# Decoding double-precision weights on VectorE alone, in an attention and maxout kernel on one core

## The chip, the cores and the metric

The kernel runs on one core of one Trainium2 chip. The metric is the device time of one execution in microseconds (us), given as the median of several executions. The engines of the core are TensorE (PE in the profile, its weight loads PEld), VectorE (DVE), ScalarE (ACT), GpSimd (POOL) and SyncE (SP, which here only issues transfers). Each runs its own instructions strictly in its own order and waits on semaphores where it needs another engine's result.

## The reference

The reference is causal attention with a bias from a running sum, and then a feed-forward layer in which the largest of three products is kept:

```python
scores = scale * np.matmul(q, k.transpose(0, 1, 3, 2))      # 8 batches, 8 heads, 576 positions, width 64
s_pos = np.maximum(s, 0.0)
cum = np.cumsum(s_pos, axis=-1)
bias = -(cum[:, :, :, None] - cum[:, :, None, :])
scores = np.where(causal, -1000000000.0, scores + np.minimum(bias, 0.0))
attn = np.exp(scores - np.max(scores, axis=-1, keepdims=True))
attn = attn / (np.sum(attn, axis=-1, keepdims=True) + 1e-09)
x = np.matmul(attn, v)                                      # heads side by side: 4608 tokens of 512
h = np.maximum(np.maximum(x @ w1, x @ w2), x @ w3)          # 512 to 768
out = h @ w_out                                             # 768 to 512
```

The four weight matrices are drawn in double precision, and lie in memory as 64-bit words.

## The kernel before

**The steps.** Attention runs in 160 steps. A step is one block of 128 queries (64 in the last block of a sequence) of one pair of heads; a visit is a run of steps of one pair. Visits 0 to 7 (two batches, four pairs) take query blocks 0 and 1, which is phase 0; so steps 0 to 15 are the even and odd steps of eight visits. Visits 8 to 15 take blocks 2, 3 and 4 of the same pairs (phase 1), and every later visit all five. In step t the engines do, in program order:

- `probs(t)`, first half: DVE takes the reciprocal `ri` (L486), ACT writes the high half `prh` of the probabilities in f16 (L502).
- `highest(t + 1)`: DVE takes the row maximum `nm` (L450) of the next step's scores. Then come the functions put down with `amid` for this step.
- `probs(t)`, second half: DVE writes the low half `prl` (L505), and SP issues two DMA transposes (L508) of `prh` and `prl` into the tiles `ph` and `pl`, from which the product with the values reads.
- the evictions of matmul results (L583, L584, L725, L728), at most one group of feed-forward matmuls, and `scores(t + 2)` on PE (L419, in one of two PSUM tiles `s`), which needs `prl` of step t to be done with its tile.
- `expo(t + 1)` on ACT (L460, L464), which gives `se`, the input of the next `ri`.
- the functions put down with `at` for this step, further feed-forward groups, and `values` (L574) of the visit that ended in the step before.

The order is written out: no engine looks for other work when the next instruction in its row has to wait.

**The weights.** 24 tiles of 128 rows by 512 doubles (18 of w1, w2, w3, 6 of w_out), 512 KB each, are loaded once (`load_w`, L187), four from SP and twenty from ACT. A tile is turned into two f16 halves in these parts, spread over the steps up to 17:

- `decode1` (ACT, L605): the high words, read as f32, times 2^-112 into a tile `t` (three buffers);
- `signs` (POOL, L609): the high words times zero, in place, which leaves only the sign bit;
- `decode2a` (DVE, L613): the low words shifted right by 29, ORed with that sign;
- `decode2b` (DVE, L620): `t` shifted left by 3, ORed with the result, which is the weight in f32;
- `gram1` and `gram2`: a bound for the scale, from all tiles of a kind;
- `decode3` (ACT, L674): the high f16 half; and `decode4`, the low one: DVE in one operation (L684) for 16 tiles, POOL in two (L681, L682) for the 8 tiles whose number is in `LOW`.

In steps 0 to 6 two tiles are decoded a step (one before step 0), in step 7 three, in steps 8 to 13 one. `decode4` of three tiles a step follows in steps 9 to 14, 16 and 17. A feed-forward group of PE (`h_group`, L711; `o_group`, L753) may be issued only in a step after its weights' `decode4`; `run_group` issues them by a budget that is worked out when the program is built, so PE's row is fixed.

**The transposed tiles.** `PT` holds `ph` and `pl` in a pool with one buffer a tag. The first eight visits take the tags `pTh0` and `pTh1` in turns (and `pTl0`, `pTl1`); later ones take the tag of their phase.

**DMA semaphores.** Eight of them (DMAHW0 to DMAHW7 in the rows below) are handed out in turns over all transfers, of SP and ACT alike. A transfer is issued only when the one that held its semaphore before has landed.

The rest of POOL's work around there is the low half of k (`qkl`, L327) and the split of the feed-forward result (`hh` L717, `hl` L718).

Of the kernel before, what the change touches and what calls it, by code (L numbers as in the profile page):

```python
# [8 lines left out]
F32 = mybir.dt.float32  # L9
F32R = mybir.dt.float32r  # L10
F16 = mybir.dt.float16
BF16 = mybir.dt.bfloat16
I32 = mybir.dt.int32
I64 = mybir.dt.int64
AF = mybir.ActivationFunctionType
ALU = mybir.AluOpType
# [5 lines left out]
def kernel(  # L22
# [9 lines left out]
    nc = tc.nc  # L32

    P = 128
    D = 64
    B, NP, _, QKV = qkv.shape
    HB, S = s.shape
    NW, _, N = wts.shape
# [6 lines left out]
    NB = qkv0.shape[0]  # L45
# [6 lines left out]
    PH = [(0, 256), (256, 320)]  # L52
# [4 lines left out]
    LOW = set(range(2, 24, 3))  # L57

    const = ctx.enter_context(tc.tile_pool(name="const", bufs=1))
# [131 lines left out]
    zero = const.tile([P, 1], F32, name="zero")  # L191
    nc.gpsimd.memset(zero, 0.0)
# [276 lines left out]
    def probs(t):  # L469
# [5 lines left out]
        if qb in (0, 2):  # L475
            PT[v, ph] = [
                att.tile(
                    [P, 4 + 4 * ph, PH[ph][1]], F16, tag=f"pT{c}{v % 2 if v < NP * NB else ph}", name=f"p{c}{t}", bufs=1
                )
                for c in "hl"  # L480
            ]
            if ph:
                PT[v, ph].append(att.tile([P, 1, P], F16, tag="tT", name=f"tT{t}"))
# [115 lines left out]
    def words(i):  # L599
        w = raw_w[i].rearrange("p (n t) -> p n t", t=2)  # L600
        return w[:, :, 0], w[:, :, 1]
# [5 lines left out]
    def signs(i):  # L607
        hi = words(i)[1]
        nc.gpsimd.tensor_tensor(out=hi, in0=hi, in1=zero.to_broadcast([P, N]), op=ALU.mult)  # L609

    def decode2a(i):
        lo, hi = (x.bitcast(I32) for x in words(i))
        nc.vector.scalar_tensor_tensor(  # L613
            out=lo, in0=lo, scalar=29, in1=hi, op0=ALU.logical_shift_right, op1=ALU.bitwise_or
        )

    def decode2b(i):
        lo = words(i)[0].bitcast(I32)
        ti = half.pop(i).bitcast(I32)
        nc.vector.scalar_tensor_tensor(  # L620
            out=lo, in0=ti, scalar=3, in1=lo, op0=ALU.logical_shift_left, op1=ALU.bitwise_or
        )
# [53 lines left out]
    def decode4(i):  # L676
        t = words(i)[0]
        w = pairs_w[i // 2][:, i % 2]
        sw = WS["u" if i < 18 else "d"]
        if i in LOW:  # L680
            nc.gpsimd.tensor_tensor(out=t, in0=t, in1=sw.to_broadcast([P, N]), op=ALU.mult)  # L681
            nc.gpsimd.tensor_tensor(out=w[:, 1], in0=t, in1=w[:, 0], op=ALU.subtract)  # L682
        else:
            nc.vector.scalar_tensor_tensor(  # L684
                out=w[:, 1], in0=t, scalar=sw, in1=w[:, 0], op0=ALU.mult, op1=ALU.subtract
            )
        fresh[i] = w.rearrange("p h (a c) -> p h a c", c=P)
# [122 lines left out]
    def at(t, f, *a):  # L810
        todo.setdefault(t, []).append((f, a))
# [15 lines left out]
    fetched = {5: -1, 7: -1, 8: 0, 9: 0, 10: 1, 11: 1, 12: 2, 13: 2, 14: 3, 15: 3, 16: 4, 17: 4}  # L827
    fetched.update({22: 5, 23: 5, 18: 5, 19: 6, 20: 6, 21: 7})
# [13 lines left out]
    parts2 = {}  # L842
    for i, t in sorted(begun.items(), key=lambda x: (x[1], x[0])):
        parts2.setdefault(t + 1, []).append(i)
    for t, ids in parts2.items():
        (amid if t >= 0 else at)(t, decode2a, ids[0])
        for i in ids[1:]:
            at(t, decode2a, i)
        for i in ids:
            at(t, decode2b, i)  # L850
# [46 lines left out]
    for i, t in sorted(begun.items()):  # L897
        at(t, decode1, i)
        at(t, signs, i)
    for n, (i, t) in enumerate(fetched.items()):  # L900
        (amid if t >= 0 and n % 2 == 0 else at)(t, load_w, i, nc.scalar.dma_start)
# [114 lines left out]
```

## Time and profile before

| what | us |
|---|---|
| median of 3 runs | 944.0 (943.08 to 945.74) |
| the profiled execution, its own time | 945.22 |
| its span, first to last instruction | 943.4 |
| PE busy | 838.6 |
| DVE busy | 582.7 |
| ACT busy | 569.4 |
| POOL busy | 386.8 |

The span is 1.8 us less than the profiled execution's time, and that time is 1.2 us above the median. In the profile's rows a group is named by source line, engine, operation and tiles; behind a stroke stand its busy time, the mean duration in ns, and the idle time of the engine just before it with what ended it.

### The profile page before, as it was taken

To read this page: it belongs to the slowest core of one execution; us is meant where nothing else is said; L and a number is where in the kernel's file an instruction comes from. 1 tells how busy PE (TensorE), PEld (TensorE's weight loads), DVE (VectorE), ACT (ScalarE), POOL (GpSimd) and SP (SyncE) were. 2 spreads that over 40 slices of the span, in tenths; PEclk is the share of its full clock that TensorE was granted. 3 is DMA by queue.
4 is the path that set the end of the run, shared out by engine and by line. 5 is a ranking of instruction groups with operands and counts; after the bars stand their busy time and mean duration, and the time that the engine had idled before them with its cause. 6 is when DMAs were issued, how large, how long until landed. Compare 5 with 4: busy or idle time off the path is not lost. (4 is left out here: it accounts for less than half of the span.)

```text
span 943.4 us, 19983 instructions
## 1 busy us (share of the span) xinstructions
PE 838.6 (89%) x7192; PEld 653.2 (69%) x7192; DVE 582.7 (62%) x1184; ACT 569.4 (60%) x1502; POOL 386.8 (41%) x592
## 2 busy tenths in 40 slices
PE   2456768887779899999999998999999999998998
PEld 2444647765556677877887777877887787776876
DVE  6897885666556575667575666576666656563111
ACT  4667566566467576676676676666667666764111
POOL 4455742222433453635453535454455435430211
PEclk9857999999899999999999999999999999999999
DMA  7974236566577678777778677787676676744000
GB/s 277 237 223 88 58 75 140 115 137 150 118 139 144 119 138 162 152 141 136 157 141 155 134 135 135 135 141 145 133 138 148 127 153 102 139 69 96 2 24 28
DMA packets 242035, 122.34 MB, mean 130 GB/s; under 512 B 217808, under 2 KB 226512, under 8 KB 241936
## 3 DMA queue, kind: packets, MB, share of 16 engines
q1 hardware_dynamic: 237904, 108.74, 58.1%
q10 hardware_dynamic: 4032, 12.32, 4.1%
q8 instruction: 57, 0.93, 0.4%
q14 instruction: 42, 0.34, 0.2%
HBM read 60.18 MB, written 9.44 MB: 74 GB/s over the span
## 5 line engine op out<-in xcount | busy, mean ns | idle before, releaser
L711 PE MATMUL pm<-x,w 128*128 128x256 f16 (+1 forms) x3456 | 462.9, 290 | 3.7 <-ACT m L725 1.7
L711 PEld LDWEIGHTS <-w 128*128 128x128 f16 x3456 | 334.2, 99 | 89.6 <-issue 4.1
L505 DVE SCALAR_TENSOR_TENSOR prl<-s,ri,prh 128x512 f16<-128x512 f32 (+3 forms) x288 | 152.8, 567 | 96.6 <-ACT prh L502 50.4
L717 POOL CAST hh<-m 128x256 f16<-128x256 f32 (+1 forms) x96 | 53.5, 557 | 351.4 <-DVE m L728 294.4
L502 ACT ACTIVATE prh<-s,ri 128x512 f16<-128x512 f32 (+3 forms) x288 | 141.8, 538 | 80.8 <-DVE ri L486 71.7
L450 DVE TENSOR_REDUCE nm<-s 128x1 f32<-128x576 f32 (+4 forms) x160 | 128.0, 800 | 49.3 <-PE s L385 28.9
L460 ACT ACTIVATE s<-s,nm 128x512 f32<-128x512 f32 (+4 forms) x288 | 151.2, 525 | 9.2 <-DVE nm L450 4.1
L753 PE MATMUL po<-hh,w 128*128 128x256 f16 (+1 forms) x768 | 150.4, 287 | 1.5 <-DVE w L684 1.5
L728 DVE SCALAR_TENSOR_TENSOR m<-pm,m 128x256 f32<-128x256 f32 (+1 forms) x192 | 87.1, 454 | 97.4 <-PE pm L711 85.0
L753 PEld LDWEIGHTS <-w 128*128 128x128 f16 x1152 | 110.4, 98 | 31.1 <-DVE w L684 2.1
L753 PE MATMUL po<-hl,w 128*128 128x320 f16 (+1 forms) x384 | 110.0, 287 | 0.9 <-POOL hl L718 0.8
L725 ACT ACTIVATE m<-pm 128x256 f32<-128x256 f32 (+1 forms) x96 | 39.1, 407 | 83.9 <-PE pm L711 80.2
L718 POOL TENSOR_TENSOR hl<-m,hh 128x256 f16<-128x256 f32 (+1 forms) x96 | 74.1, 772 | 7.8
L583 ACT ACTIVATE x<-av 128x256 f16<-128x256 f32 (+1 forms) x64 | 26.3, 410 | 78.6 <-PE av L574 77.9
L138 POOL CAST l<-kb 64x576 fp32r<-64x576 f32 x48 | 32.3, 673 | 100.6 <-PE s L394 75.6
L761 ACT ACTIVATE o<-po,os 128x256 f32<-128x256 f32 (+1 forms) x64 | 31.9, 498 | 65.5 <-PE po L753 50.0
L169 POOL TENSOR_TENSOR l<-raw,h 64x576 fp32r<-64x576 f32 x48 | 68.2, 1422 | 7.2 <-ACT h L155 6.0
L584 DVE SCALAR_TENSOR_TENSOR x<-av,x 128x256 f16<-128x256 f32 (+1 forms) x64 | 29.1, 454 | 59.0 <-ACT x L583 58.9
L574 PEld LDWEIGHTS <-vh 128*64 128x64 f16 x832 | 45.0, 112 | 24.6 <-issue 17.1
L574 PE MATMUL av<-pl,vh 128*64 128x320 f16 (+3 forms) x384 | 56.3, 279 | 5.7 <-DMA pl<-prl 5.6
L379 PE MATMUL s<-h 128*128 128x128 f32 (+1 forms) x192 | 53.7, 361 | 8.4 <-DVE prl L505 7.0
L574 PE MATMUL av<-ph,vh 128*64 128x320 f16 (+3 forms) x384 | 57.5, 287 | 0.6 <-DMA ph<-prh 0.6
(142 smaller groups left out, 1148.2 us busy)
## 6 DMA issues: line engine op xcount, KB each, us to landing
raw<-in_qk_dram SPq DMA_DIRECT2D x96, 304.0 KB, 4.7
r<-in_w_dram ACTq DMA_DIRECT2D x20, 512.0 KB, 4.9
rv<-in_qkv_dram SPq DMA_DIRECT2D x32, 320.0 KB, 3.4
out_dram<-o SPq DMA_DIRECT2D x32, 160.0 KB, 2.0
out_dram<-o SPq DMA_DIRECT2D x32, 128.0 KB, 2.3
raw<-in_qkv_dram SPq DMA_DIRECT2D x8, 480.0 KB, 3.9
ph<-prh SPq DMA_TRANSPOSE x192, 3.3
pl<-prl SPq DMA_TRANSPOSE x192, 2.8
```

The lines of the kernel that those rows point to most:

```text
L169: nc.gpsimd.tensor_tensor(out=l[far, QP:V0], in0=raw[far, QP:V0], in1=h[far, QP:V0].bitcast(F32), op=ALU.subtract)
L379: nc.tensor.matmul(ps[:, j, :nk], lhsT=w[:, qs], rhs=w[:, QP:QP + nk], start=(x == "h"), stop=False, skip_group_check=True,)
L450: nc.vector.tensor_reduce(out=nm, in_=sc, axis=AX.X, op=ALU.max, negate=True)
L460: nc.scalar.activation(out=sc, in_=sc, func=AF.Exp, bias=nm[:, j:j + 1], accum_out=sm[:, j:j + 1])
L502: nc.scalar.activation(out=hi, in_=src, func=AF.Copy, scale=sc)
L505: nc.vector.scalar_tensor_tensor(out=lo, in0=src, scalar=sc, in1=hi, op0=ALU.mult, op1=ALU.subtract)
L574: nc.tensor.matmul(av[j * D:(j + 1) * D, c0:nq], lhsT=lt, rhs=rt, start=(n < 2), stop=(n >= len(todo) - 2), skip_group_check=True,)
L711: nc.tensor.matmul(pm[:, :nq], lhsT=w[:, wt, kt, :], rhs=xt, start=(n == 0), stop=(n == 3 * NKT - 1))
L717: nc.gpsimd.tensor_copy(out=st["hh"][:, ft, :nq], in_=m1[:, :nq])
L718: nc.gpsimd.tensor_tensor(out=st["hl"][:, ft, :nq], in0=m1[:, :nq], in1=st["hh"][:, ft, :nq], op=ALU.subtract)
L728: nc.vector.scalar_tensor_tensor(out=m1[:, :nq], in0=pm[:, :nq], scalar=HSC, in1=m1[:, :nq], op0=ALU.mult, op1=ALU.max)
L753: nc.tensor.matmul(pm[:, :nq], lhsT=W[18 + ft][:, wt, dt, :], rhs=st[ht][:, ft, :nq], start=(n == 0), stop=(n == 3 * NFT - 1),)
```

## The change

`signs` and the constant `zero` go, and POOL takes no part in the decode any more. `decode1` stays. `decode2a` and `decode2b` become three operations of DVE: `shift` (`t` shifted left by 3, in place, one input), `low_bits` (the low words shifted right by 29, ORed into `t`) and `sign` (the sign bit of the high words ORed with `t`, written over the low words). All tiles of a step go through one operation before the next: the shifts stand between `nm` and `prl` (`amid`), the other two behind, where before the first tile's `decode2a` alone stood ahead of `prl`. `decode4` is one DVE operation for all 24 tiles. The weight loads are issued earlier, three a step from the start, and always at the step's end. The tiles `ph` and `pl` get one buffer a phase in all visits.

```diff
-    LOW = set(range(2, 24, 3))
...
-    zero = const.tile([P, 1], F32, name="zero")
-    nc.gpsimd.memset(zero, 0.0)
...
-                att.tile(
-                    [P, 4 + 4 * ph, PH[ph][1]], F16, tag=f"pT{c}{v % 2 if v < NP * NB else ph}", name=f"p{c}{t}", bufs=1
-                )
-                for c in "hl"
+                att.tile([P, 4 + 4 * ph, PH[ph][1]], F16, tag=f"pT{c}{ph}", name=f"p{c}{t}", bufs=1) for c in "hl"
...
-    def signs(i):
-        hi = words(i)[1]
-        nc.gpsimd.tensor_tensor(out=hi, in0=hi, in1=zero.to_broadcast([P, N]), op=ALU.mult)
-
-    def decode2a(i):
+    def shift(i):
+        ti = half[i].bitcast(I32)
+        nc.vector.tensor_scalar(out=ti, in0=ti, scalar1=3, scalar2=None, op0=ALU.logical_shift_left)
+
+    def low_bits(i):
+        lo, ti = words(i)[0].bitcast(I32), half[i].bitcast(I32)
+        nc.vector.scalar_tensor_tensor(
+            out=ti, in0=lo, scalar=29, in1=ti, op0=ALU.logical_shift_right, op1=ALU.bitwise_or
+        )
+
+    def sign(i):
         lo, hi = (x.bitcast(I32) for x in words(i))
...
-            out=lo, in0=ti, scalar=3, in1=lo, op0=ALU.logical_shift_left, op1=ALU.bitwise_or
+            out=lo, in0=hi, scalar=-(2 ** 31), in1=ti, op0=ALU.bitwise_and, op1=ALU.bitwise_or
...
-        if i in LOW:
-            nc.gpsimd.tensor_tensor(out=t, in0=t, in1=sw.to_broadcast([P, N]), op=ALU.mult)
-            nc.gpsimd.tensor_tensor(out=w[:, 1], in0=t, in1=w[:, 0], op=ALU.subtract)
-        else:
-            nc.vector.scalar_tensor_tensor(
-                out=w[:, 1], in0=t, scalar=sw, in1=w[:, 0], op0=ALU.mult, op1=ALU.subtract
-            )
+        nc.vector.scalar_tensor_tensor(
+            out=w[:, 1], in0=t, scalar=WS["u" if i < 18 else "d"], in1=w[:, 0], op0=ALU.mult, op1=ALU.subtract
+        )
...
-    fetched = {5: -1, 7: -1, 8: 0, 9: 0, 10: 1, 11: 1, 12: 2, 13: 2, 14: 3, 15: 3, 16: 4, 17: 4}
-    fetched.update({22: 5, 23: 5, 18: 5, 19: 6, 20: 6, 21: 7})
+    fetched = {5: -1, 7: -1, 8: -1, 9: 0, 10: 0, 11: 0, 12: 1, 13: 1, 14: 1, 15: 2, 16: 2, 17: 2}
+    fetched.update({22: 4, 23: 4, 18: 5, 19: 6, 20: 6, 21: 7})
...
+    for t, ids in together.items():
+        for f in (shift, low_bits, sign):
+            for i in ids:
+                (amid if f is shift and t >= 0 else at)(t, f, i)
...
-        at(t, signs, i)
-    for n, (i, t) in enumerate(fetched.items()):
-        (amid if t >= 0 and n % 2 == 0 else at)(t, load_w, i, nc.scalar.dma_start)
+    for i, t in fetched.items():
+        at(t, load_w, i, nc.scalar.dma_start)
```

In DVE's row, step 4 reads like this before, from its `ri` to the next one (r is a weight tile, t its rescaled high words):

```order
L486 RECIPROCAL ri_505<-se_478 128x2
L450 TENSOR_REDUCE nm_464<-s_463 128x2
L613 SCALAR_TENSOR_TENSOR r_299<-r_299 128x512
L505 SCALAR_TENSOR_TENSOR prl_508<-s_378,ri_505,prh_507 128x128 x2
L613 SCALAR_TENSOR_TENSOR r_309<-r_309 128x512
L620 SCALAR_TENSOR_TENSOR r_299<-t_495,r_299 128x512
L620 SCALAR_TENSOR_TENSOR r_309<-t_498,r_309 128x512
L354 SCALAR_TENSOR_TENSOR vl_490<-st_139,inv_0_233,vh_489 128x2x128
L486 RECIPROCAL ri_587<-se_534 128x2
```

The same step in DVE's row after the change (line numbers are those of the changed file):

```order
L480 RECIPROCAL ri_505<-se_481 128x2
L447 TENSOR_REDUCE nm_467<-s_466 128x2
L603 TENSOR_SCALAR t_499<-t_499 128x512
L603 TENSOR_SCALAR t_501<-t_501 128x512
L499 SCALAR_TENSOR_TENSOR prl_508<-s_379,ri_505,prh_507 128x128 x2
L607 SCALAR_TENSOR_TENSOR t_499<-r_295,t_499 128x512
L607 SCALAR_TENSOR_TENSOR t_501<-r_297,t_501 128x512
L614 SCALAR_TENSOR_TENSOR r_295<-r_295,t_499 128x512
L614 SCALAR_TENSOR_TENSOR r_297<-r_297,t_501 128x512
L351 SCALAR_TENSOR_TENSOR vl_494<-st_137,inv_0_231,vh_493 128x2x128
L480 RECIPROCAL ri_587<-se_533 128x2
```

Four operations on two weight tiles have become six; none of them reads anything of POOL's.

In ACT's row, this is the end of step 2 and the beginning of step 3 before, where DMA rows on r are weight loads and those on rv loads of values:

```order
L605 ACTIVATE t_425<-r_252 128x512
L605 ACTIVATE t_428<-r_264 128x512
L187 DMA r_431<-in_w_dram 128x512
L502 ACTIVATE prh_448<-s_315,ri_446 128x2x128 x2
L187 DMA r_454<-in_w_dram 128x512
L583 ACTIVATE x_0_460<-av_0_433 128x256
L460 ACTIVATE s_378,sm_475<-s_378,nm_379 128x128 x2
L464 ACTIVATE se_478<-sm_475 128x2
L112 DMA rv_485<-in_qkv_dram 128x256
L112 DMA rv_487<-in_qkv_dram 128x256
```

And the same place in ACT's row after:

```order
L599 ACTIVATE t_427<-r_248 128x512
L599 ACTIVATE t_429<-r_250 128x512
L186 DMA r_431<-in_w_dram 128x512
L186 DMA r_433<-in_w_dram 128x512
L186 DMA r_435<-in_w_dram 128x512
L496 ACTIVATE prh_452<-s_314,ri_450 128x2x128 x2
L577 ACTIVATE x_0_463<-av_0_437 128x256
L457 ACTIVATE s_379,sm_478<-s_379,nm_380 128x128 x2
L461 ACTIVATE se_481<-sm_478 128x2
L111 DMA rv_489<-in_qkv_dram 128x256
```

Three loads (tiles 15, 16 and 17) now stand in a row ahead of `prh`; before, one stood ahead of it and one behind (tiles 13 and 14).

SP's row holds the same transfers in the same order; its waits differ. These are the four transposes of visit 1 (steps 2 and 3) and the first of visit 2 (step 4) before, each with the semaphores it waits for:

```order
L508 DMA_TRANSPOSE ph_362<-prh_366 128x2x128 [waits DMAHW6_49,Activation_49]
L508 DMA_TRANSPOSE pl_363<-prl_367 128x2x128 [waits DMAHW0_49,DVE_49,PE_49]
L508 DMA_TRANSPOSE ph_362<-prh_448 128x4x128 [waits DMAHW3_49,Activation_49]
L508 DMA_TRANSPOSE pl_363<-prl_449 128x4x128 [waits DMAHW4_49,DVE_49]
L508 DMA_TRANSPOSE ph_503<-prh_507 128x2x128 [waits DMAHW1_49,DMAHW2_49,PE_49,Activation_49]
```

And after:

```order
L502 DMA_TRANSPOSE ph_364<-prh_368 128x2x128 [waits DMAHW4_49,DMAHW3_49,DMAHW6_49,PE_49,Activation_49]
L502 DMA_TRANSPOSE pl_365<-prl_369 128x2x128 [waits DMAHW7_49,DMAHW6_49,DVE_49]
L502 DMA_TRANSPOSE ph_364<-prh_452 128x4x128 [waits DMAHW0_49,Activation_49]
L502 DMA_TRANSPOSE pl_365<-prl_453 128x4x128 [waits DMAHW1_49,DVE_49]
L502 DMA_TRANSPOSE ph_503<-prh_507 128x2x128 [waits DMAHW4_49,DMAHW0_49,DMAHW7_49,PE_49,Activation_49]
```

The first transpose of visit 1 now waits for PE, that is for the last matmul of `values` of visit 0, because both visits write the same buffer. In step 4 the wait for PE stood there before too, but for the visit before the last; now it is for the last one, whose `values` stands at the end of step 4 in PE's row.

More of the change, by code (lines that the diff above doesn't have):

```diff
@@ L605, in decode1 @@
         nc.scalar.activation(out=half[i], in_=words(i)[1], func=AF.Copy, scale=2.0 ** -112)
-    def signs(i):
-        hi = words(i)[1]
-        nc.gpsimd.tensor_tensor(out=hi, in0=hi, in1=zero.to_broadcast([P, N]), op=ALU.mult)
-    def decode2a(i):
-        lo, hi = (x.bitcast(I32) for x in words(i))
-        nc.vector.scalar_tensor_tensor(
-            out=lo, in0=lo, scalar=29, in1=hi, op0=ALU.logical_shift_right, op1=ALU.bitwise_or
-        )
-    def decode2b(i):
-        lo = words(i)[0].bitcast(I32)
+    def shift(i):
[7 more added lines that the diff above has]
+    def sign(i):
+        lo, hi = (x.bitcast(I32) for x in words(i))
         ti = half.pop(i).bitcast(I32)
         nc.vector.scalar_tensor_tensor(
-            out=lo, in0=ti, scalar=3, in1=lo, op0=ALU.logical_shift_left, op1=ALU.bitwise_or
+            out=lo, in0=hi, scalar=-(2 ** 31), in1=ti, op0=ALU.bitwise_and, op1=ALU.bitwise_or
         )
@@ L678, in decode4 @@
         w = pairs_w[i // 2][:, i % 2]
-        sw = WS["u" if i < 18 else "d"]
-        if i in LOW:
-            nc.gpsimd.tensor_tensor(out=t, in0=t, in1=sw.to_broadcast([P, N]), op=ALU.mult)
-            nc.gpsimd.tensor_tensor(out=w[:, 1], in0=t, in1=w[:, 0], op=ALU.subtract)
-        else:
-            nc.vector.scalar_tensor_tensor(
-                out=w[:, 1], in0=t, scalar=sw, in1=w[:, 0], op0=ALU.mult, op1=ALU.subtract
-            )
+        nc.vector.scalar_tensor_tensor(
+            out=w[:, 1], in0=t, scalar=WS["u" if i < 18 else "d"], in1=w[:, 0], op0=ALU.mult, op1=ALU.subtract
+        )
         fresh[i] = w.rearrange("p h (a c) -> p h a c", c=P)
@@ L841 @@
         at(first[v] + 1 if v else -2, vscale2, scale_of(v))
-    parts2 = {}
+    together = {}
     for i, t in sorted(begun.items(), key=lambda x: (x[1], x[0])):
[L844 to L850, printed above, removed]
+        together.setdefault(t + 1, []).append(i)
+    for t, ids in together.items():
+        for f in (shift, low_bits, sign):
+            for i in ids:
+                (amid if f is shift and t >= 0 else at)(t, f, i)
     for i, t in split.items():
@@ L896 @@
         at(t, decode3, i)
-    for i, t in sorted(begun.items()):
+    for i, t in begun.items():
         at(t, decode1, i)
-        at(t, signs, i)
-    for n, (i, t) in enumerate(fetched.items()):
-        (amid if t >= 0 and n % 2 == 0 else at)(t, load_w, i, nc.scalar.dma_start)
+    for i, t in fetched.items():
+        at(t, load_w, i, nc.scalar.dma_start)
     at(1, spread, 1)
```

## The prediction

> **What bounds the kernel now.** I read PE's row of the page's slices first (busy tenths of 40 equal slices), then the busy time of two windows.
>
> ```profile
> PE   2456768887779899999999998999999999998998
> ...
> 12.00:142.00 130.00, 77.02 (x630) 59.73 (x630) 112.11 (x224) 82.47 (x222) 68.95 (x67) 0.82 0.57 146
> 142.00:943.00 801.00, 758.36 (x6550) 591.00 (x6550) 465.07 (x950) 483.12 (x1273) 312.25 (x495) 0.99 0.64 124
> ```
>
> A window's row gives its length, then the busy time of PE, PEld, DVE, ACT and POOL, the granted clock, the DMA share and GB/s. From 142 us on PE is busy for 758 of 801 us: matmul work bounds that part, and the change doesn't touch it. From 12 to 142 us, which is where the weights are decoded, PE is busy for 77 of 130 us and DVE for 112. PE's row is fixed when the program is built, and nothing after 142 us refers to a time, so what the first part gains or loses is passed on whole. Who waits for whom from 12 to 142 us:
>
> ```profile
> ACT prh L502 <- DVE ri L486: 26.0, 12, 5.7
> PE s L419 <- DVE prl L505: 22.4, 7, 5.7
> ...
> DVE r L613 <- POOL r L609: 11.4, 9, 3.4
> ...
> DVE prl L505 <- ACT prh L502: 2.4, 2, 1.7
> ```
>
> Columns: total, times, longest. ACT and PE wait for DVE; DVE itself waits for little but POOL's sign operation. So DVE's row sets the pace of this part, and 130 us are 112 of work, 11.4 of waiting for POOL and small waits.
>
> **The change part by part.** Its operations in that window, and their shortest, median and longest durations:
>
> ```profile
> L613 DVE SCALAR_TENSOR_TENSOR r<-r 128x512 int32<-128x512 int32 x24 | 23.8, 994 | 11.4 <-POOL r L609 11.4
> L620 DVE SCALAR_TENSOR_TENSOR r<-t,r 128x512 int32<-128x512 int32 x24 | 16.9, 734 | 0.1
> L684 DVE SCALAR_TENSOR_TENSOR w<-r,swu,w 128x512 f16<-128x512 f32 x12 | 13.1, 1132 | 0.0
> L684 DVE SCALAR_TENSOR_TENSOR w<-r,swd,w 128x512 f16<-128x512 f32 x4 | 5.6, 1442 | 0.0
> L330 DVE SCALAR_TENSOR_TENSOR qkl<-raw,qkh 128x256 fp32r<-128x256 f32 x4 | 3.7, 918 | 0.0
> L330 DVE SCALAR_TENSOR_TENSOR qkl<-st,qkh 128x256 fp32r<-128x256 f32 x3 | 1.2, 415 | 0.0
> ...
> L613 DVE SCALAR_TENSOR_TENSOR r<-r x24: 676/694/1520, 16.6 to 105.2; 128x512 int32<-128x512 int32 x24
> L620 DVE SCALAR_TENSOR_TENSOR r<-t,r x24: 673/680/1343, 18.2 to 107.8; 128x512 int32<-128x512 int32 x24
> L684 DVE SCALAR_TENSOR_TENSOR w<-r,swu,w x12: 740/1158/1639, 78.1 to 117.5; 128x512 f16<-128x512 f32 x12
> ```
>
> *The wait.* `shift` needs only ACT's `t`, so DVE's 11.4 us of waiting for POOL go. Step 10 shows one such wait, and DVE's row from one `ri` to the next (start, length, idle before in brackets):
>
> ```profile
> 79.75 0.16 DVE L486 RECIPROCAL ri<-se 128x2 f32<-128x2 f32 x1
> 82.17 1.51 DVE L613 SCALAR_TENSOR_TENSOR r<-r 128x512 int32<-128x512 int32 x1 [1.67 <-POOL r L609]
> 84.13 1.12 DVE L620 SCALAR_TENSOR_TENSOR r<-t,r 128x512 int32<-128x512 int32 x1
> 86.50 1.65 DVE L354 SCALAR_TENSOR_TENSOR vl<-rv,inv,vh 128x256 f16<-128x256 f32 x2
> 88.07 0.15 DVE L486 RECIPROCAL ri<-se 128x2 f32<-128x2 f32 x1
> ```
>
> The last `ri` begins at 88.07, 80 ns ahead of the end of L354 at 88.15: of operations that follow each other, each costs some 80 ns less than its length.
>
> *The slow half.* The same operation on the same shape takes 676 ns or 1520. On POOL one operation of one shape, L681, has a mean of 1270 or 1042 ns in its two rows below. I read this as DVE and POOL holding each other up when both are at work. Above the shortest there are 24 x (994 - 676) = 7.6 us on L613, 24 x (734 - 673) = 1.5 on L620, 12 x (1132 - 740) + 4 x (1442 - 740) = 7.5 on L684, and 4 x (918 - 415) = 2.0 on `qkl`, by its two rows: 18.6 us. POOL's work in the window is 68.95 us, and what goes is this:
>
> ```profile
> L609 POOL TENSOR_TENSOR r<-r,zero 128x512 f32<-128x512 f32 x24 | 28.2, 1190 | 34.2 <-ACT t L605 34.1
> L682 POOL TENSOR_TENSOR w<-r,w 128x512 f16<-128x512 f32 x8 | 11.2, 1398 | 0.6
> L681 POOL TENSOR_TENSOR r<-r,swu 128x512 f32<-128x512 f32 x6 | 7.6, 1270 | 0.0
> L681 POOL TENSOR_TENSOR r<-r,swd 128x512 f32<-128x512 f32 x2 | 2.1, 1042 | 1.2 <-ACT w L674 1.2
> ```
>
> That is 49.1 of 68.95 us, 71%. I take the hold-ups to go with POOL's time: 0.71 x 18.6 = 13.2 us; the bounds are 0 and 18.6.
>
> *The added operations.* `low_bits` and `sign` have two inputs and the shape of L613 and L620, and replace them one for one: nothing. Eight more L684 cost 8 x 0.66 = 5.3 us (740 ns less the 80). For `shift` the trace has no row: a 32-bit shift with one input. The nearest rows are these:
>
> ```profile
> L239 DVE TENSOR_TENSOR cc<-c_t,cc 64x576 fp32r<-64x576 f32 x1 | 0.8, 751 | 0.0
> L234 DVE TENSOR_SCALAR r_t<-s_t 64x576 f32<-64x576 f32 x1 | 0.4, 441 | 0.0
> ```
>
> On 576 columns a one-input operation took 441 ns where a two-input one took 751. From 415 (256 columns, two inputs) to 676 (512) a column costs 1.02 ns, on a fixed part of 154. So L239 ran at one column per 1.02 ns, and L234 at half of that. By L234 a shift of 512 columns takes 154 + 261 = 415 ns, 0.34 us with the overlap; by L613, 0.60. I take 0.34, as it is a TENSOR_SCALAR: 24 x 0.34 = 8.2 us, and 14.4 as the upper bound. The Trainium skill ("VectorE: DVE Perf Modes", the perf-mode tier table) gives fp32 tensor_scalar in SBUF twice the rate and makes it depend on operand size and place, not on the operation; by that rule the sum is the one I take, and at the plain rate it would be 6.2 us more. A page of the same skill speaks against the change: "SBUF — State Buffer" (Who interferes with whom) has a VectorE operation in such a two-port mode, as well as one with two SBUF inputs, fully blocked by a GpSimd operation that reads SBUF. By that rule the 1520 beside 676 is a whole POOL operation waited out, and the trace agrees for two inputs; for `shift` no run here shows it yet, and what it would do is part of rival 1.
>
> DVE's sum: -11.4 - 13.2 + 5.3 + 8.2 = -11.1 us.
>
> *What is late next.* PE's rows beside step 10:
>
> ```profile
> 84.35 0.45 PE L419 MATMUL s<-qkh 64*128 64x128 f32 x2 [3.18 <-ACT w L674]
> 85.56 3.89 PE L711 MATMUL pm<-x,w 128*128 128x256 f16 x24
> 90.00 1.49 PE L711 MATMUL pm<-x,w 128*128 128x256 f16 x12
> ```
>
> DVE's 8.3 us of that step lose 1.67 of waiting, 0.8 on L613, 0.4 on L620, 0.8 on `vl` (L354), and gain 0.34 and 0.66: 5.6. PE's work of that step, from 84.35 to 91.4, is 7.1 us without a gap, so PE ends this step and takes back 1.5 us. In step 3 and 4 it is ACT that stands still, for issues:
>
> ```profile
> 38.55 1.63 ACTq L112 DMA_DIRECT2D rv<-in_qkv_dram  x2
> 40.23 0.51 ACT L349 ACTIVATE vh<-st,inv 128x256 f16<-128x256 f32 x1 [1.48 <-issue]
> 40.31 0.36 ACTq L187 DMA_DIRECT2D r<-in_w_dram  x1
> ```
>
> One weight load more a step in steps 0 to 2 costs ACT 0.36 us each; ACT's wait for `ri` covers it, but at one place, where ACT is already last: 0.3 us. Each transfer also waits until the one that held its DMA semaphore has landed. The bunched loads bring those waits forward along with the landings; I add nothing, and up to 1.5 us at the upper end, one more wait like the 1.48.
>
> *One buffer a phase.* In steps 2, 4, ... 14 the first transpose now waits for `values` of the visit before, at the end of the same step in PE's row. Queued behind it on SP are the step's other transpose, those of the next step and the loads `raw` of visits 6 and 7; who waits for it is `prh` two steps on, which has two buffers, and the next `values`. The phase-1 visits work this way already, and visit 8 shows it at its worst, since it shares visit 7's buffer (this wait goes). SP's waits from 12 to 142 us, ACT's from 145 to 260, and how long transposes took to land from 14 to 60:
>
> ```profile
> SPq L508 <- PE av L574: 11.7, 1, 11.7
> ...
> ACT prh L502 <- DMA ph<-prh: 7.9, 6, 2.7
> ...
> DMA to landing us min/median/max: 3.4/4.7/7.1
> ```
>
> The 11.7 us of SP are covered by the two steps. The price is what `prh` waits: 0 to 2.7 us for each of seven visits, 1.3 in the mean of phase 1. Steps 2 and 3 are the shortest pair, with `values` of visit 0 in them:
>
> ```profile
> 30.84 0.15 DVE L486 RECIPROCAL ri<-se 128x2 f32<-128x2 f32 x1
> 37.02 0.22 PE L574 MATMUL av<-ph,vl 128*64 128x128 f16 x2
> 40.74 0.15 DVE L486 RECIPROCAL ri<-se 128x2 f32<-128x2 f32 x1
> ```
>
> `values` ends at 37.2, 6.4 us into the pair; a transpose issued then lands 4.7 later, 11.1 us into it, and `prh` of step 4 asks for it after 9.9: up to 1.2 us late here, and in time in longer pairs. I take 0, because the wait of visit 8 that goes balances it.
>
> The sum: -11.1 + 1.5 + 0.3 = -9.3 us. On the profiled execution that is 945.2 - 9.3 = 935.9; that execution is 1.2 us above the median of 944.0, so the forecast is 944.0 - 9.3 = 934.7 us.
>
> **The rivals.** (1) The shift costs more than 0.34 us. At the plain rate it is 6.2 us more on DVE. DVE is then last in step 10 and at ACT's places too, so the 1.8 us are not lost besides: -11.1 + 6.2 = -4.9, 939.1 us. A shift held up by what is left of POOL's work is a smaller case: POOL is still at work for 19.9 of 130 us, 15%, and a hold-up is 1520 - 676 = 844 ns at most, so 24 x 0.15 x 0.5 = 1.8 us, 936.5. For both: no row of an integer shift; against: L234, and that POOL is mostly idle then.
>
> (2) PE takes the gain of the middle steps. In the step shown it already does. PE is idle for 8.2 of 32 us there, from 80 to 112 us:
>
> ```profile
> 80.00:112.00 32.00, 23.79 (x207) 19.11 (x206) 28.51 (x46) 22.13 (x57) 20.70 (x19) 0.88 0.41 88
> ```
>
> If feed-forward groups and scores leave half of that gap in place, these four steps give 4.1 us; the forecast has some 7 there (2.7 a step at most, by step 10, less the 1.5 and the shorter waits of the others). The sum is then -6.3: some 938. Against it: PE's gaps there end with `prl`.
>
> (3) The one buffer costs what it costs in phase 1. At 1.3 us for each of seven visits the 9.1 us eat the gain: 943.8, no change. At the longest, 2.7 each, 18.9 us, it is 9.6 slower: 953.6. It decides from 9.3 / 7 = 1.33 us a visit. For it: transposes land slowest, up to 7.1 us, just while the weight loads are bunched. Against it: in phase 1 PE is full and `values` comes late; here PE idles.
>
> **How the numbers follow.** Forecast 0.61; rival 1 0.17 (0.12 at the plain rate, 0.05 held up); rival 2 0.09; rival 3 0.13, of which 0.07 near its mean and 0.06 beyond. About 2.8 us, 0.3%, is what a measurement can tell from no change. Faster: 0.87 from the first three, less 0.03 for the ends of rivals 1 and 2 that come within 2.8 us: 0.84. Same: 0.07 + 0.03 = 0.10. Slower: 0.06. The range: if all 18.6 us of hold-ups go (5.4 more) and nothing is late next, up to 16.5 us are gained; I go to 15, 929. The other end takes rival 1's 939.1 with 1.5 us of ACT's issues and 1.2 us at each of two visits of rival 3: 943.
>
> **What would show it.** Right: DVE waits for POOL in no step of the decode; L684's successor has a mean near 750 ns on DVE; `shift` about 415; PE's continuous part begins 8 to 11 us earlier, with the window after it unchanged. Wrong: `shift` near 680 ns (rival 1); PE without gaps from 80 to 112 us at a small gain (rival 2); ACT's `prh` waiting for the transposes of `ph` in steps 4 to 14, over a microsecond each (rival 3); ACT waiting for issues in steps 1 to 4 longer than 1.5 us.

## The result and the profile after

The changed kernel takes 934.99 us in the median of 5 executions (930.61 to 937.13), the kernel before 944.0 in the same session: a ratio of 0.989 with a 95% interval of 0.9844 to 0.9935. A second session gave 935.3 us and 0.9895 (0.986 to 0.9929). The medians differ by 9.0 us; the ratio stands for 10.4 us, its interval for 6 to 15. The forecast was 934.7 us, a gain of 9.3.

PE's row of the slices in the page of the changed kernel:

```profile
PE   2567788988789899999999999999999999998998
```

Its first eight digits add up to 52, where they added up to 46 before: more of PE's work falls into the first fifth of the span. Two windows of it, with columns as in the prediction; the first is 8 us shorter than the one shown of before, because the decode ends earlier:

```profile
12.00:134.00 122.00, 79.14 (x622) 61.62 (x621) 108.56 (x254) 82.12 (x219) 23.57 (x27) 0.77 0.60 157
134.00:928.00 794.00, 754.72 (x6560) 589.50 (x6558) 465.90 (x951) 484.29 (x1276) 312.92 (x495) 0.99 0.64 125
```

DVE is busy for 108.6 of 122 us where it was for 112.1 of 130. It executes 254 instructions there instead of 224 and still works less. POOL's busy time fell from 68.95 to 23.57 us. The changed operations in the first window (busy us, mean ns, idle before):

```profile
L614 DVE SCALAR_TENSOR_TENSOR r<-r,t 128x512 int32<-128x512 int32 x24 | 16.5, 721 | 0.2
L607 DVE SCALAR_TENSOR_TENSOR t<-r,t 128x512 int32<-128x512 int32 x24 | 15.8, 687 | 0.0
L673 DVE SCALAR_TENSOR_TENSOR w<-r,swu,w 128x512 f16<-128x512 f32 x18 | 14.6, 862 | 0.0
L603 DVE TENSOR_SCALAR t<-t 128x512 int32<-128x512 int32 x24 | 9.4, 422 | 2.7 <-ACT t L599 2.7
L673 DVE SCALAR_TENSOR_TENSOR w<-r,swd,w 128x512 f16<-128x512 f32 x6 | 4.3, 777 | 0.0
```

And the shift's shortest, median and longest duration, from the instructions of its tile:

```profile
L603 DVE TENSOR_SCALAR t<-t x24: 408/416/550, 15.4 to 99.3; 128x512 int32<-128x512 int32 x24
```

The shift takes 416 ns; the prediction took 415 from a row on another shape and another type. All 24 `decode4` on DVE take 18.9 us (14.6 + 4.3), where 16 of them took 18.7 before. What DVE waits for in the window (total, times, longest):

```profile
DVE prl L499 <- ACT prh L496: 3.8, 6, 1.8
DVE t L603 <- ACT t L599: 2.7, 2, 2.3
DVE prl L499 <- ACT s L457: 1.7, 1, 1.7
DVE qr L266 <- ACT kb L263: 1.4, 1, 1.4
```

POOL is gone from this list, where it stood with 11.4 us. But ACT has taken part of its place: `t` wasn't in the list before, and `prh` stood at 2.4.

To see where the time went I cut the span at three marks: the start of `ri` of step 0, of step 9 and of step 18. The windows between them, first of the kernel before, then of the changed one:

```profile
19.90:70.50 50.60, 26.59 (x212) 21.37 (x214) 46.16 (x101) 32.74 (x97) 23.27 (x20) 0.73 0.86 227
70.50:140.40 69.90, 47.52 (x403) 36.74 (x399) 58.76 (x109) 45.09 (x112) 41.32 (x43) 0.85 0.32 72
```

```profile
17.60:68.90 51.30, 27.53 (x212) 22.05 (x214) 47.16 (x120) 33.42 (x97) 7.09 (x5) 0.71 0.84 232
68.90:133.50 64.60, 48.84 (x396) 37.90 (x393) 56.34 (x122) 45.16 (x112) 15.84 (x22) 0.79 0.41 87
```

Step 0 begins 2.3 us earlier (DVE had waited 1.6 us for POOL ahead of it), steps 0 to 9 last 0.7 us longer, steps 9 to 18 last 5.3 us less: 6.9 us by step 18. The two spans differ by 14.6 us (943.4 and 928.8), so 7.7 us of that difference lie behind step 18, where the change alters no instruction. The first experiment takes up these 7.7 us.

### The profile page after: what moved, and what is told of

Same layout as the page of the kernel before. It is cut to its first block, busy times and chain, and to the rows that moved or that the text cites. A ratio compares the mean times of both kernels' runs of the same rounds, so it can differ in the third digit from the quotient of the medians.

```text
span 928.8 us, 19936 instructions
## 1 busy us (share of the span) xinstructions
PE 837.1 (90%) x7192; PEld 653.6 (70%) x7192; DVE 579.7 (62%) x1216; ACT 570.2 (61%) x1502; POOL 342.1 (37%) x551
## 5 line engine op out<-in xcount | busy, mean ns | idle before, releaser
L700 PE MATMUL pm<-x,w 128*128 128x256 f16 (+1 forms) x3456 | 457.8, 288 | 2.7 <-DVE m L717 1.2
L742 PE MATMUL po<-hh,w 128*128 128x256 f16 (+1 forms) x768 | 152.6, 290 | 0.0
L568 PE MATMUL av<-ph,vh 128*64 128x320 f16 (+3 forms) x384 | 57.4, 286 | 1.6 <-DMA ph<-prh 1.6
```

Source lines behind the costliest of these rows:

```text
L568: nc.tensor.matmul(av[j * D:(j + 1) * D, c0:nq], lhsT=lt, rhs=rt, start=(n < 2), stop=(n >= len(todo) - 2), skip_group_check=True,)
L700: nc.tensor.matmul(pm[:, :nq], lhsT=w[:, wt, kt, :], rhs=xt, start=(n == 0), stop=(n == 3 * NKT - 1))
L742: nc.tensor.matmul(pm[:, :nq], lhsT=W[18 + ft][:, wt, dt, :], rhs=st[ht][:, ft, :nq], start=(n == 0), stop=(n == 3 * NFT - 1),)
```

## The experiments

My theory was that of the prediction: DVE paces the program up to step 18, the decode alone changes its row, by taking away waits for POOL and hold-ups, and the other two parts cost nothing. Its rivals were a price for the one buffer, a part of the loads in the gain, and a pace set by something other than DVE. All times are medians. The median of the kernel before differs by a us from session to session, so I compare the ratios to it; a difference "by the medians" or "by the ratios" is one to the second session of the changed kernel (935.3 us, 0.9895). The stages, in us, are read from one profiled execution of each kernel with the same three marks; "rest" is the span less the start of step 18.

| kernel | ratio to before (95%) | step 0 at | steps 0-9 | steps 9-18 | rest |
|---|---|---|---|---|---|
| before | 1 | 19.9 | 50.6 | 69.9 | 803.0 |
| changed, first session | 0.989 (0.9844-0.9935) | 17.6 | 51.3 | 64.6 | 795.3 |
| changed, again | 0.9895 (0.986-0.9929) | 17.7 | 50.7 | 64.7 | 804.8 |
| decode alone | 0.9889 (0.9848-0.9929) | 17.7 | 48.6 | 65.4 | 804.3 |
| two buffers a phase | 0.9904 (0.9869-0.9939) | 17.6 | 51.4 | 65.5 | 798.8 |
| loads as before | 0.9896 (0.9861-0.9932) | 17.7 | 53.9 | 63.6 | 798.9 |
| other two parts alone | 1.0001 (0.9978-1.0024) | 20.8 | 51.4 | 70.3 | 801.7 |
| POOL makes eight halves | 0.9963 (0.9932-0.9995) | 17.5 | 50.6 | 69.3 | 803.0 |
| idle multiplications on POOL | 0.9983 (0.9954-1.0011) | 19.7 | 56.8 | 65.6 | 802.3 |
| third operation waits for POOL | 1.002 (1.0-1.004) | 19.9 | 57.4 | 67.1 | 799.9 |
| shift with two inputs | 0.9956 (0.9931-0.9981) | 17.9 | 53.8 | 65.3 | 800.3 |
| weights one by one | 0.9932 (0.9907-0.9958) | 17.8 | 55.2 | 63.6 | 802.9 |
| without low bits | 0.9895 (0.9862-0.9928) | 16.9 | 53.8 | 61.1 | 795.4 |
| without low bits, decode alone | 0.9807 (0.9759-0.9855) | 17.0 | 44.6 | 61.5 | 801.2 |

**The changed kernel again.** No edit.

> The changed kernel once more, unaltered. If the whole gain sits in the first 140 us (my theory), the reciprocal of step 18, which marks the end of the continuous part, starts near 133.5 us again (140.4 us in the kernel before), and the stretch from there to the end of the span lasts between 794 and 801 us, whichever run it is: the 7.7 us by which the first two traces differ behind step 18 are a matter of the run. If the change also made the stretch behind step 18 shorter, it lasts 794 us again and the ratio to the kernel before is near 0.985 rather than 0.990.

935.3 us (929.62 to 939.76). Step 18 starts at 133.1 us, and the rest lasts 804.8 us, against 795.3 in the first execution of the same program, and 803.0 in the kernel before. I had expected 794 to 801. So the rest differs by 9.5 us between two executions of one program, and the 7.7 us can't be put down to the change. One stretch in which the two executions differ is 220 to 320 us; first the first execution of the changed kernel, then its second (clock third from the right):

```profile
220.00:320.00 100.00, 82.18 (x648) 58.56 (x649) 56.21 (x114) 59.53 (x155) 40.07 (x64) 0.93 0.69 131
```

```profile
220.00:320.00 100.00, 80.85 (x590) 56.56 (x589) 54.10 (x108) 55.72 (x143) 37.34 (x60) 0.88 0.68 130
```

The second was granted a clock of 0.88 there and has 590 matmuls on record instead of 648 in the same 100 us. The kernel before had 0.93 in that stretch and a rest of 803.0, so the clock in this one stretch isn't the whole of it. What sets the clock there wasn't tried.

**The decode alone**, with two buffers a phase and the loads as before:

```diff
-  tag=f"pT{c}{ph}"
+  tag=f"pT{c}{v % 2 if v < NP * NB else ph}"
-  fetched = {5: -1, 7: -1, 8: -1, 9: 0, 10: 0, 11: 0, 12: 1, 13: 1, 14: 1, 15: 2, 16: 2, 17: 2}
+  fetched = {5: -1, 7: -1, 8: 0, 9: 0, 10: 1, 11: 1, 12: 2, 13: 2, 14: 3, 15: 3, 16: 4, 17: 4}
...
```

> The changed decode alone: two buffers a phase for the transposes and the loads as before. My theory: the decode carries all of the gain, so the time is within 2.8 us of the changed kernel (about 935 us) and step 18's reciprocal starts near 133.5 us. If one buffer a phase costs what a wait for values costs (1.3 us a visit), this is faster than the changed kernel by up to 9 us, near 926 us. If the bunched loads carry part of the gain, it is slower, at 937 to 940 us.

935.03 us, ratio 0.9889: the decode carries the whole gain. Step 18 starts at 131.7 us.

**Two buffers a phase**, the first of these two edits alone.

> The changed kernel with the two buffers a phase of before. My theory: the transposes' wait of 7 x 1.9 us on SyncE's queue is hidden, so the time is the same (within 2.8 us). The rival by which one buffer costs 1.3 us a visit: faster by 9 us, near 926 us; at a third of that price, 3 us.

935.75 us, ratio 0.9904: no difference from the changed kernel that the intervals show, and none near 9 us. The wait itself is real, and hidden. SP's largest wait in the window 12 to 134 us of the changed kernel:

```profile
SPq L502 <- PE av L568: 41.8, 7, 13.4
```

Seven visits, 41.8 us together, 6.0 each and not the 1.9 that I had taken, in place of one of 11.7 before. ACT's waits in that window hold none for the transposes of `ph`.

**The loads as before**, the second edit alone.

> The changed kernel with the load schedule of before (two weights a step, half of the issues in the middle of a step). My theory: no weight is waited for in either schedule, so the time is the same (within 2.8 us), and ScalarE's waits at the issues are within 1.5 us. The rival by which bunching loads earlier helps, since the decode then never meets a late weight: slower by 3 us or more, with waits for r tiles in steps 4 to 8. A rival by which bunching holds ScalarE up at its issues: faster by 1.5 us.

934.98 us, ratio 0.9896: no difference. One part of the expectation failed: in this execution ACT waited 3.0 us at an issue for a transfer and DVE 3.7 us for `prl`'s transfer, more than the 1.5 us that I had as a bound. Such waits come in other executions too, in steps 3 to 5, at one place each: 2.6 us on ACT in the changed kernel's second, 2.9 with two buffers, none with the decode alone or in the changed kernel's first execution. Steps 0 to 9 are longest here (53.9 us), where these waits are longest, and shortest with the decode alone (48.6); the medians show no difference.

**The other two parts alone**, on the kernel before.

> The kernel before with the other two parts of the change alone: one buffer a phase for the transposes, and the loads bunched; the decode with GpSimd as before. My theory: nothing within 2.8 us of the kernel before (944 us). The rival by which one buffer a phase costs 1.3 us a visit: 953 us.

942.79 us beside 943.16, ratio 1.0001 (0.9978 to 1.0024). The rival of 1.3 us a visit is excluded from this side as well.

**POOL makes eight halves.** The set `LOW` of before and its two POOL operations come back; the decode of the bits stays on DVE.

```diff
+  if i in LOW:
+      nc.gpsimd.tensor_tensor(out=t, in0=t, in1=sw.to_broadcast([P, N]), op=ALU.mult)
+      nc.gpsimd.tensor_tensor(out=w[:, 1], in0=t, in1=w[:, 0], op=ALU.subtract)
+  else:
...
```

> The changed kernel, but the second halves of weights 2, 5, 8, ... 23 are again made by two GpSimd operations each. By my terms this gives VectorE back 8 x 0.66 = 5.3 us and lays on it the hold-ups of decode4 (12 x 392 ns + 4 x 702 ns = 7.5 us in the trace of before, times 0.71 = 5.3 us): no difference within 2.8 us, with decode4 above 1.1 us a piece, and step 18 within 2 us of 133.5. Rival, that the hold-ups cost less than I counted: faster than the changed kernel by up to 5 us, near 930 us. Rival, that TensorE and its GpSimd work, not VectorE, pace steps 9 to 18: slower by 3 us or more.

939.67 us, ratio 0.9963, with an interval (0.9932 to 0.9995) that lies above that of the changed kernel's second session and touches that of its first: 4.4 us slower by the medians, 6.4 by the ratios. My terms, which balance at nothing, were wrong here, and the first rival was wrong in its sign. The second rival has the number but not the reason. The window of steps 9 to 18:

```profile
68.10:137.40 69.30, 49.91 (x405) 38.41 (x401) 60.48 (x114) 45.22 (x112) 36.09 (x38) 0.81 0.38 81
```

And `decode4` in the groups of DVE:

```profile
L679 DVE SCALAR_TENSOR_TENSOR w<-r,swu,w 128x512 f16<-128x512 f32 x12 | 14.4, 1239 | 0.0
L679 DVE SCALAR_TENSOR_TENSOR w<-r,swd,w 128x512 f16<-128x512 f32 x4 | 5.6, 1448 | 0.0
```

DVE is busy for 60.5 of 69.3 us and idle for 8.8; in the changed kernel it was 56.3 of 64.6, idle for 8.3. So DVE still sets the pace, and with eight operations fewer it is busy for 4.1 us more. Sixteen `decode4` beside POOL take 20.0 us, where 24 without it take 18.9, and the rest of the 4.1 us is on the neighbours (the four `qkl` there 782 ns on average instead of 481, the shift 576 instead of 415). Handing POOL a third of that work made DVE slower.

**Idle multiplications on POOL.** Twenty of before's 24 multiplications, into a spare buffer.

```diff
...
+  nc.gpsimd.tensor_tensor(out=spare_out, in0=words(i)[1], in1=zero.to_broadcast([P, N]), op=ALU.mult)
...
```

> The changed kernel and, in addition, 20 of the 24 GpSimd multiplications of before (upper word times zero, at the same places of GpSimd's queue), into a buffer that nobody reads; the output is not touched. Nobody waits for them, so only the hold-ups come back. My theory: in steps 0 to 8 VectorE and GpSimd slow each other again by 7.8 us as in the trace of before (18 x 330 + 18 x 45 + 2 x 523 ns), times 0.71 = 5.5 us, so step 9's reciprocal starts near 74 us instead of 69 and the time is near 940.5 us. Rival, that only the waits for GpSimd counted: 935 us, step 9 at 69.

942.76 us, ratio 0.9983: nearly all of the gain is gone (7.5 us by the medians, 8.3 by the ratios), by work that nobody waits for. Steps 0 to 9 of this kernel:

```profile
19.70:76.50 56.80, 27.35 (x212) 21.86 (x214) 54.46 (x120) 33.39 (x97) 22.93 (x19) 0.81 0.75 197
```

Its shift (L611) and its `low_bits` (L615), shortest, median and longest:

```profile
L611 DVE TENSOR_SCALAR t<-t x24: 409/418/1258, 15.8 to 107.2; 128x512 int32<-128x512 int32 x24
L615 DVE SCALAR_TENSOR_TENSOR t<-r,t x24: 674/682/1525, 16.5 to 109.8; 128x512 int32<-128x512 int32 x24
```

The same number of operations keeps DVE busy for 54.5 us instead of 47.2 in these steps. Step 9 starts at 76.5 us, 7.6 later than in the changed kernel; I had 5.5. One step shows it, the two shifts and the two `low_bits` of step 1, and POOL beside them (start, length). The fourth row is the next pair of shifts, in step 2, while POOL stands idle:

```profile
24.34 1.73 DVE L611 TENSOR_SCALAR t<-t 128x512 int32<-128x512 int32 x2
25.99 0.86 DVE L501 SCALAR_TENSOR_TENSOR prl<-s,ri,prh 128x256 f16<-128x256 f32 x2
26.77 2.19 DVE L615 SCALAR_TENSOR_TENSOR t<-r,t 128x512 int32<-128x512 int32 x2
...
33.60 0.75 DVE L611 TENSOR_SCALAR t<-t 128x512 int32<-128x512 int32 x2
...
24.57 5.29 POOL L607 TENSOR_TENSOR junk<-r,zero 128x512 f32<-128x512 f32 x4
```

Two shifts take 1.73 us beside POOL and 0.75 without it. `prl` between them reads its scores from PSUM and only one input of that size from SBUF, and took 0.86 us for two, no longer than elsewhere (two of that shape took 0.87 us in step 3 of the changed kernel).

**The third operation waits for POOL.** All 24 multiplications in place, ahead of `sign`.

> The changed kernel with all 24 GpSimd multiplications of before in place, so that the third VectorE operation of the decode waits for them; the output is the same. Hold-ups as in the run with idle multiplications (6 to 7 us for 24) and in addition a wait at the third operation, which stands 1.1 us a tile later than the one that waited in before: 2 to 5 us of before's 11.4. My theory: 943 to 947 us, waits for L609's work at the sign operation, step 9 near 76 us. Rival, that waits alone count: 937 to 940 us. If neither counts: 935 us.

944.9 us, ratio 1.002: the number is as expected, one of its two reasons isn't. The view of DVE's waits has no entry for POOL, and DVE stands idle for 0.7 us in all before `sign` (0.2 in the changed kernel), where I had 2 to 5 us of waiting: `sign` stands behind two other operations. So the time comes from hold-ups: DVE is busy for 55.6 of the 57.4 us of steps 0 to 9. Steps 9 to 18, too, are longer here (67.1 us) than with the idle multiplications (65.6), which leave out the last four weights.

**The shift with two inputs.** Same result, `scalar_tensor_tensor` instead of `tensor_scalar`.

```diff
...
-  nc.vector.tensor_scalar(out=ti, in0=ti, scalar1=3, scalar2=None, op0=ALU.logical_shift_left)
+  nc.vector.scalar_tensor_tensor(out=ti, in0=ti, scalar=3, in1=izero.to_broadcast([P, N]),
+      op0=ALU.logical_shift_left, op1=ALU.bitwise_or)
...
```

> The changed kernel with the shift written as an operation of two inputs (shift, then or with a zero of one column spread over the row), the same result. One of them should last 676 ns instead of 416: 24 x 0.26 = 6.2 us more on VectorE, 20 of the 24 by step 9. My theory that VectorE paces this part at rate one: step 9 starts 5 us later (74 us) and the time is near 941 us. Rival, that TensorE takes half of what VectorE gains in the middle steps: 938 us. Rival, that the slow part is elsewhere: 935 us.

939.23 us, ratio 0.9956 (0.9931 to 0.9981), above the changed kernel's intervals, one of which ends at 0.9935 and so overlaps a little. The shift:

```profile
L605 DVE SCALAR_TENSOR_TENSOR t<-t,izero x24: 674/678/817, 15.4 to 103.3; 128x512 int32<-128x512 int32 x24
```

Steps 0 to 9:

```profile
17.90:71.70 53.80, 27.18 (x210) 21.84 (x212) 51.68 (x119) 33.45 (x97) 8.64 (x4) 0.81 0.77 220
```

The price is 262 ns an operation, as expected, and DVE is busy for 4.5 us more in steps 0 to 9. They last 2.5 us longer than in the changed kernel, 3.1 longer than in its second execution. So, with one execution each, more than half of what DVE does more goes into the length of these steps, where I had expected all of it. The time is 3.9 us longer by the medians and 5.8 by the ratios, between the rival's 3 and the theory's 6.

**The weights one by one** instead of in turns:

```diff
-  for f in (shift, low_bits, sign):
-      for i in ids:
+  for i in ids:
+      for f in (shift, low_bits, sign):
...
```

Only the first weight's shift stays ahead of `prl`; the second's moves behind it.

> The changed kernel with the three operations of one weight behind each other instead of in turns over a step's weights. If an operation that needs its forerunner's result costs nothing more than one that doesn't, the time is the same (within 2.8 us). Rival: dependent operations can't overlap; in the trace neighbours that don't depend start some 80 ns earlier than their duration says, and 24 x 2 x 0.08 = 3.8 us would come on top, near 939 us, step 9 three us later.

937.69 us, ratio 0.9932 (0.9907 to 0.9958). That interval overlaps the changed kernel's. The stage points the rival's way:

```profile
17.80:73.00 55.20, 27.34 (x210) 22.12 (x212) 50.31 (x119) 32.92 (x97) 3.73 (x4) 0.69 0.81 217
```

DVE is busy for 50.3 us in steps 0 to 9 instead of 47.2. That is 3.1 us more, where 20 of the 24 weights that lose two overlaps of 80 ns each make 3.2. But this execution also has 2.3 us of DVE waiting for a transfer. That the turns gain about 3 us is likely and not shown.

**Without the low bits.**

```diff
-  for f in (shift, low_bits, sign):
+  for f in (shift, sign):
```

> The changed kernel without the second decode operation (the three lowest bits of each weight's upper half are left out): 24 x 0.69 = 16.5 us less on VectorE, 20 of the 24 by step 9. If VectorE alone paces steps 0 to 9, they shrink by 20 x 0.61 = 12 us and the time falls by 14 us, to 921 us. Rival: the transfers, whose share is 0.84 of the 51.3 us of steps 0 to 9 (43 us of work), take over, so at most 8 us go there and 1 to 2 behind: 925 to 927 us, with waits for the weights' transfers.

933.42 us, ratio 0.9895: no gain over the changed kernel from some 16 us less on DVE. Steps 0 to 9:

```profile
16.90:70.70 53.80, 26.94 (x212) 22.31 (x214) 36.76 (x101) 32.88 (x98) 3.18 (x4) 0.75 0.88 226
```

The waits from 12 to 70 us of DVE, ACT and SP:

```profile
DVE prl L499 <- DMA pl<-prl: 7.5, 3, 4.4
...
ACT prh L496 <- DMA ph<-prh: 6.5, 2, 3.5
...
SPq L502 <- PE av L568: 12.9, 4, 5.0
SPq L502 <- DMA pl<-prl: 11.5, 1, 11.5
```

DVE works for 36.8 us instead of 47.2, and steps 0 to 9 are no shorter (53.8 us after 51.3); what steps 9 to 18 gain (61.1 after 64.6) is mostly lost there. DVE and ACT now wait for the transposes before they can overwrite `prl` and `prh`: 7.5 and 6.5 us, the signs of the prediction's rival 3. Two explanations were left: there is too much to transfer, or the transposes are late by the one buffer and the bunched loads.

**Without the low bits, on the decode alone.** The same edit with two buffers a phase and the loads as before.

> Again without the second decode operation, but on the changed decode alone: two buffers a phase for the transposes and the loads as before. With one buffer and bunched loads, steps 0 to 9 lasted 53.8 us without that operation (51.3 with it), VectorE busy 36.8, the transfers' share 0.88 (47 us). Theory, that the amount of transfers is what comes late next: with the changed decode alone the share was 0.94 of 48.6 us (46 us), so steps 0 to 9 stay between 46 and 50 us and the time is 930 to 935 us. Rival, that it is the one buffer and the bunched loads, priced at nothing, that hold the transposes once VectorE is faster: steps 0 to 9 shrink by VectorE's 10 us to 40 to 44 us and the time falls to 923 to 927 us, without VectorE's waits for transposes (7.5 us with one buffer).

924.98 us, ratio 0.9807 (0.9759 to 0.9855), which lies wholly below that with one buffer and bunched loads (0.9862 to 0.9928). Steps 0 to 9:

```profile
17.00:61.60 44.60, 27.80 (x212) 22.92 (x214) 36.34 (x101) 32.29 (x98) 3.26 (x5) 0.97 1.04 275
```

DVE's three longest waits from 12 to 70 us:

```profile
DVE t L606 <- ACT t L602: 5.1, 4, 2.2
DVE qr L266 <- ACT kb L263: 2.3, 1, 2.3
DVE x L581 <- ACT x L580: 2.0, 2, 1.6
```

DVE's busy time is the same, 36.3 us, but these steps last 44.6 us instead of 53.8, and DVE waits for no transfer. The theory is wrong and the rival right, with 44.6 us for its 40 to 44. The amount of transfers wasn't the limit: the DMA engines' mean share was 0.88 in the slower kernel and is 1.04 here (the share comes out above 1, so I use it only to compare). What held the transposes is one of the two parts that show no cost as long as DVE is late, or both together. Which of them wasn't tried with this shorter decode.

## Why the prediction was right, and where its steps were not

**The bound** was right: DVE paces the part up to step 18. The idle multiplications show it best, as they give PE and ACT no work and cost 7.6 us by step 9.

**The work on DVE** was right in most of its terms, and fell by more than their sum. The forecast's terms for it (-13.2, +5.3 and +8.2) come to +0.3 us; up to step 18 DVE's busy time fell by 2.6 us (110.62 to 108.05, worked out below). By the rows, L613 and L620 (23.8 + 16.9 us) became L607 and L614 (15.8 + 16.5): 8.4 us less, where 0.71 of their hold-ups was 6.5. `decode4` is at 18.9 after 18.7 us with eight more: +0.2, where +5.3 and 0.71 of 7.5 balance at nothing; but its means are 862 and 777 ns, not near the 750 that I named as a sign. The four `qkl` of 256 columns that were held up fell from 3.7 to 1.7 us, by 2.0 where the forecast had 1.4, and two of 384 columns that it left out from 2.0 to 1.1. The shift cost what the forecast had. Its row says 9.4 us, but a row counts in full the 80 ns in which an operation overlaps with the next group's; from the start of two shifts to the start of what follows it is 0.67 us, 0.34 each (step 3 of the changed kernel; start, length):

```profile
34.37 0.75 DVE L603 TENSOR_SCALAR t<-t 128x512 int32<-128x512 int32 x2
35.04 0.87 DVE L499 SCALAR_TENSOR_TENSOR prl<-s,ri,prh 128x256 f16<-128x256 f32 x2
```

The Trainium skill ("VectorE: DVE Perf Modes", the perf-mode tier table) gives a `tensor_scalar` on fp32 data in SBUF twice the plain rate. The trace agrees for an integer shift: 416 ns against 678 with two inputs are 262 and 524 ns beyond the prediction's fixed part of 154.

**The hold-ups** were the most doubtful term, and the runs bear it out and raise it. The multiplications alone, with no one waiting, cost 7.5 to 8.3 us of time where I had 5.5, and POOL's share of `decode4` costs 4.4 to 6.4 us net where I had nothing. The Trainium skill ("SBUF — State Buffer", Who interferes with whom) has a VectorE operation in two-port mode, or with two SBUF inputs, blocked while a GpSimd operation reads SBUF. The trace agrees for both sorts that they are held up: the shift goes from 418 to 1258 ns at most beside POOL, an operation with two inputs from 682 to 1525, some 840 ns more each. It doesn't show what the prediction read out of 1520 beside 676, a whole POOL operation waited out, since the shortest of these multiplications lasts 1038 ns. What makes up the difference wasn't tried.

**The wait for POOL** went as forecast, 11.4 us. The step that failed, though the total was right, is the one behind it, what is late next. I named PE in step 10 and ACT's issues, 1.8 us together. Up to step 18, DVE's idle time fell by 4.3 us only: before, from 12 us on, 128.4 us less 110.62 busy (5.70 ahead of step 0, 46.16, 58.76), 17.8; after, 121.5 less 108.05 (4.55, 47.16, 56.34), 13.5. Of the 11.4 us some 7 came back as other waits, most of them for ACT: 2.7 for `t`, 1.7 for `s`, 1.4 more for `prh`. POOL's operation had itself waited 34.1 us for `t` by its row in the prediction; I take it that its place in the chain had hidden that ACT is only just ahead. So step 18 starts 6.9 us earlier in this pair (2.6 of work, 4.3 of idle time), not 8 to 11. Over all profiled executions it starts at 133.6 us in the mean of the five with the new decode and nothing else changed on DVE, and at 141.4 in the mean of the two with the old one: 7.8 us. The gain of 9.0 us in the medians and these marks agree within what the measurement can tell. That 9.0 is so near to 9.3 is partly luck: too much was hoped for from the waits, and too little from the work.

**Rival 2** (the middle steps) was right about its place and not about its reason. From the start of step 10 to that of step 14 it took 32.7 us before and takes 29.8 after:

```profile
79.75:112.48 32.73, 24.52 (x213) 19.72 (x212) 29.24 (x48) 22.38 (x58) 21.18 (x20) 0.88 0.40 86
77.65:107.47 29.82, 24.77 (x216) 20.10 (x215) 28.85 (x56) 21.51 (x56) 8.59 (x9) 0.84 0.34 94
```

That is a gain of 2.9 us, below the rival's 4.1 and the forecast's 7. PE didn't fill the gap, as the rival had it: it is busy for 24.8 of the 29.8 us, DVE for 28.9. The forecast had worked out step 10 and taken it for all four. In step 10 DVE's 5.6 us were right, and the 1.5 us that PE was to take back didn't come (`ri` of step 10 and of step 11 in the changed kernel):

```profile
77.65 0.16 DVE L480 RECIPROCAL ri<-se 128x2 f32<-128x2 f32 x1
83.27 0.16 DVE L480 RECIPROCAL ri<-se 128x2 f32<-128x2 f32 x1
```

The step lasts 5.62 us after 8.32. The other three together last 24.2 after 24.4. In those DVE had waited for POOL for 1.5 us only, and with a third `decode4` and the shift it is busy for 23.3 us there after 22.6. The rest of the gain came ahead of step 0 and behind step 14.

**Rival 1** falls with the 416 ns; held up by what is left of POOL's work, the shift's longest was 550. **Rival 3** falls at this length of the decode, by three comparisons: two buffers, the decode alone, and the other two parts alone. They exclude its 9 us; a cost below some 3 us, half the width of their intervals, they can't exclude. But my price of nothing had a condition that I didn't write beside it: it holds while DVE is later than the transposes. With 10 us less on DVE in steps 0 to 9, the one buffer and the bunched loads take 9.2 us of these steps (53.8 against 44.6, one execution each) and some 8 us of the time.

**The window after step 18** was to be unchanged. Its length varies by 9.5 us between two executions of one program, so a single pair of traces can't show it either way; the marks ahead of it can.

## What to carry to other kernels

Work that is given to GpSimd to relieve VectorE can cost VectorE more than it saves, as POOL's eight halves did here, and work that nobody waits for can do so too, as the idle multiplications show. To find it, compare the shortest and the mean duration of the same VectorE operation, and test with GpSimd work that no one reads. Before a wait is counted as gained, look at what the engine that was waited for had itself been waiting for. Before a gain in one step is taken for its neighbours, look whether they have the same waits. A buffer or a schedule that is measured at nothing is so under the present bound; measure it again, with the other parts, once the bound has moved.

## What the runs showed of the hardware that was not expected

- Beside GpSimd multiplications a one-input VectorE shift on int32 data, 128 x 512, grew from 418 ns in the median to 1258 at most, and a two-input operation from 682 to 1525. Both grew by the same 840 ns or so, less than the shortest of those multiplications lasted (1038).
- A GpSimd multiplication of 128 x 512 lasted 1038 to 1370 ns in the kernel with the idle ones, and the twenty of them, 22 us of GpSimd time, most of it in steps 0 to 9, added 7.3 us to VectorE's busy time in these steps.
- In the stretch from 220 to 320 us the granted clock was 0.93 in one execution of the changed kernel and 0.88 in another, and the time behind step 18 was 795.3 and 804.8 us.
